# Gated linear attention and expert mix on one core: second-layer weight loads asked for one step sooner, and x tiles' rooms lent to the staging ring

## The chip, the cores and the metric

The kernel runs on one core of one Trainium2 chip. The metric is device time in microseconds (us) of one execution. Before the change it is 2355.21 us, the median of three runs that lie between 2354.76 and 2355.55 us.

The core has a matrix engine (PE, with its weight loads shown apart as PEld), a vector engine (DVE), an activation engine (ACT), a general engine (POOL) and a sync engine (SP). Here SP does nothing but issue DMA transfers, strictly in the order of its instructions: a transfer that has to wait for an engine holds all transfers behind it.

## The reference, cut to what matters

The input `x` is 2048 tokens by 512. Two results are mixed token by token with a sigmoid gate.

```python
g = sigmoid((x * gate_w).sum(-1, keepdims=True))
a = linear_attention(x, wqkv, wo)          # 32 heads of 16
gates = softmax(x @ w_gate)                # 8 experts, all 8 are kept (top 8 of 8)
b = sum(gates[:, e] * (silu(x @ w1[e]) @ w2[e]) for e in range(8))   # w1: 512x1792, w2: 1792x512
return g * a + (1 - g) * b
```

All of it is float32. Nearly all of the arithmetic is in the two products of the experts.

## The kernel before, in words

**Arithmetic.** Each float32 operand is split into a high part and a low remainder, and a product is made of three matmuls (high by high, high by low, low by high): `mm3`, lines 57 to 60, so lines 58, 59 and 60 carry almost all PE work. Both layers use a seven-product scheme for two-by-two blocks in place of eight products; the products are called P1 to P7 and run in the order P1, P7, P2, P4, P6, P5, P3.

**Stages.** First `keys` (the keys and values of the attention, the sums of x that the scheme needs). Then one long loop in `experts`, over slots `u` from 0 to 869. Slot `u` belongs to group `g = u // 7` and step `k = u % 7`. In a slot PE does the first layer's product of group g (`up`: six matmuls into the PSUM tiles `a`, `b` or `c`) and, from slot 58 on (`LAG` = 58), one tick `n = u - 58` of the second layer (`tick`: six matmuls into the PSUM tiles `p`). Slots before 58 hold the first layer alone, and these are the "first stage" in what follows. A group is one pair of 128-column blocks of an expert's first layer; there are 116 groups: the experts for the first half of the tokens (58 groups with two of attention queries), then the same for the second half.

**Preparing weights.** For the first half of the tokens, `prep(g + 1, k)` splits the raw weights `rm` of the next group. The first layer's operands go to the tiles `o`. The second layer's operands are prepared four pieces a group, named by `n` = 0 to 3, into staging tiles: ACT writes the high half (`high2`, and `first(0)` for piece 0), DVE the low half (`low2`, line 219; line 249 for piece 0), and SP stores them to DRAM (`stash`, line 186, `w2stash<-ws`). Pieces 0 and 1 are begun at k = 1, piece 2 at k = 5 and piece 3 at k = 6; piece 0 is stored at k = 2, piece 1 at k = 3, piece 2 at k = 6, and piece 3 at the next group's k = 0. In the trace ACT's part is line 63 `ws<-rm`.

The staging tiles come from a ring of two rooms, tag `ws`. A room can be written again only when the stores of its last piece have landed. While `u < LAG - 8` = 50, pieces 0 to 2 are put into the rooms of the tiles `ho` instead (they appear as `wx`), which the second layer doesn't need yet (`m.spare`, and `ws_tile` in `prep`).

**Loading them back.** `load_w2(i)` (line 782, `w<-w2stash`, 512 KB) brings the two operands of ticks 2i and 2i + 1 into one tile `w`. Until slot 824 (`NU + 12`) these tiles have three rooms, so tile i takes the room of tile i - 3. The condition in the loop asks for tile i at the end of tick 2i - 4. The transfer waits on SP for the last matmul that reads tile i - 3. That matmul is in tick 2i - 5, or in tick 2i - 4 where item 2i - 5 is the first or the sixth of its product (`STEPS`: in these places a tick takes half of two items).

**The order of the work.** It is written out by hand: within a slot `other()` (preparing, splitting, loads of raw weights) is issued ahead of `mid()` (the tick and its evictions), and the loads of `w` follow at the end of the slot. Each engine's queue keeps that order.

**Other users of the rooms in question.** The tag `xs` has two rooms. The two tiles of x(3,1) hold them in `keys`. In the loop, `high` takes one for every sixth hidden operand (n = 5, 11, ...; issued from slot 59 on), and `load_wb` one for each expert's gate row (from slot 74 on).

**The turn to the second half.** In groups 57 and 58 (about 1120 to 1150 us) SP also brings back fourteen x tiles of 512 KB (`x_next`, line 698, `n<-xstash`), and from there on raw weights are the smaller tiles `rs`.

Of the kernel before, what the change touches and what calls it, by code (L numbers as in the profile page):

```python
# [42 lines left out]
def gated_mix_kernel(ctx: ExitStack, tc: tile.TileContext, xT, x, wk, wv, wqkv_q, wo, wm, out):  # L43
# [89 lines left out]
    weights(m)  # L133
    keys(m)
    experts(m, misc)


# [440 lines left out]
def experts(m, misc):  # L578
# [6 lines left out]
    NU = 7 * NG  # L585

    LAG = 44 + 14
# [3 lines left out]
    END = m.A[1].t0  # L591
# [4 lines left out]
    def ho_tile(name):  # L596
        return hp.tile([P, 2, TB], F32R, name=name, tag="ho", bufs=5)

    def out_tile(name):
        return hp.tile([P, TB], F32, name=name, tag="ot", bufs=4)  # L600

# [25 lines left out]
    def spill():  # L627
        while spills and spills[0][0] < m.now:
            _, dst, src, to = spills.pop(0)
            m.phi_last(dst, src)  # L630
            nc.gpsimd.dma_start(to, dst)
# [92 lines left out]
    def differ(u):  # L724
        if u % 7 == 1 and 7 < u < NU + 7 and groups[u // 7 - 1][0].e < E:
            t12, t22 = (raw[u // 7 - 1, f, 1] for f in range(2))
            v.tensor_sub(t12, t22, t12)
        for pairs, offs in ((NPAIR, (None, 6, 15, 29)), (2, (-3, -1, 1, 5))):
            for kind, off in enumerate(offs):
                if off is None or not 0 <= u - LAG - off < END:  # L730
                    continue
                part, prod, q = place(u - LAG - off)
                if part.n == pairs and prod == "P1":
                    difference(kind, part, q)
# [3 lines left out]
    def high(n):  # L738
        part, prod, q = place(n)
        s = blocks(part, q)[SRC[prod]]  # L740

        if END <= n < END + 7:
            h = m.x_tile(f"ho{n}")
        elif END + 7 <= n < END + 10:
            h = [r_tile(f"ho{n}{c}", F32R) for c in range(2)]
        elif n < END and n % 6 == 5:
            h = m.x_tile(f"ho{n}", "xs")
        else:
            h = ho_tile(f"ho{n}")
        if not isinstance(h, list):  # L750
            h = [h[:, c] for c in range(2)]
        act_copy(h[0], s)
        hop[n] = h, s

    def low_h(n):
        h, s = hop[n]
        v.tensor_sub(h[1], s, f32(h[0]))  # L757
        hop[n] = h
# [90 lines left out]
    def tick(n):  # L849
        part, prod, k = place(n)  # L850
        first = prod in ("P1", "P7")
        for q, sub in STEPS[part.n][k]:
            i = n - k + q
            if q == 0 and first:
                pb[BANK[prod], sub] = ps_tile(f"p{n}_{sub}", "dn")
            w = w2s[i // 2][:, i % 2]
            ds = slice(sub * P, (sub + 1) * P)
            h = hop[i]
            assert not isinstance(h, tuple)
            mm3(pb[bank_of(part, prod), sub], w[:, 0, ds], w[:, 1, ds], h[0], h[1], q == 0 and first, q == part.n - 1)  # L860
        if k >= part.n - 2:
            evict(part, prod, k - part.n + 2)
# [87 lines left out]
    def queries_load(i):  # L950
        if i % 2 == 0:
            Q.az = m.raw_tile(f"az{i}", F32R)
            Q.z = Q.az[:, :2 * KT * NH].rearrange("p (c f) -> p c f", c=KT)
            Q.spread = Q.az[:, 2 * KT * NH:2 * KT * NH + D].rearrange("p (c f) -> p c f", c=KT)
            Q.un = Q.az[:, 2 * KT * NH + D:2 * KT * NH + 3 * D].rearrange("p (j t) -> p j t", j=2)
            nc.sync.dma_start(f32(Q.az[:, :2 * KT * NH]), m.zcd)
            nc.sync.dma_start(f32(Q.az[:, 2 * KT * NH:2 * KT * NH + D]), m.spd)
        Q.d = m.raw_tile(f"pq{i}").rearrange("p (c t) -> p c t", c=KT)
        for c in range(KT):
            nc.sync.dma_start(Q.d[:, c], m.pqd[i // 2, i % 2, c])  # L960
# [27 lines left out]
    def queries_last(i, s):  # L988
        if 0 <= s < KT:
            if s == 0:  # L990
                Q.ps = ps_tile(f"dn{i}", "a")
            for j in range(2):
                nc.tensor.matmul(Q.ps[:2 * NH, :], Q.z[:, s], Q.un[:, j], start=(s == 0 and j == 0),
                                 stop=(s == KT - 1 and j == 1))
        elif 14 <= s < 14 + KT:
            Q.ps = ps_tile(f"n{i}_{s}", "a")
            nc.tensor.matmul(Q.ps, Q.spread[:, s - 14], Q.un[:, 0], start=True, stop=True)
# [34 lines left out]
    def rows_first(i, k):  # L1032
        if k == 0 and i % NTT == 0:
            W.acc = m.raw_tile(f"acc{i}").rearrange("p (c t) -> p c t", c=KT)
            W.r = m.raw_tile(f"row{i}").rearrange("p (c t) -> p c t", c=KT)
            for dt in range(KT):
                nc.sync.dma_start(W.acc[:, dt], m.acct[0, i // NTT, dt])
                sums[0, dt, i // NTT] = W.acc[:, dt]
        elif k == 2:
            W.ps = ps_tile(f"o0{i}", "a")  # L1040
            turn(W.ps, 0, i, range(KT), True)
        elif k == 4:
            rows_out(W.ps, 0, i, W.r[:, i % NTT])
# [47 lines left out]
    loaded, highs, lows = 3, 0, 0  # L1091
    ROWS0 = 105
    for u in range(LAG + NTICK):
        m.now = u
        n = u - LAG
        g, k = divmod(u, 7)


        query = [(i, n - part.t0) for i, part in enumerate(m.beside) if -3 <= n - part.t0 < 20]

        def mid():
            if n >= 0:
                tick(n)
            for i, s in query:
                queries_last(i, s)
            if 0 <= g - ROWS0 < NHT and k == 2:
                rows_first(g - ROWS0, k)

        m.spare = ho_tile if u < LAG - 8 else None

        def other():
            nonlocal lows, highs
            if k == 0:
                if u > 0:
                    prep(g, 7)
                m.load(g + 2)
            prep(g + 1, k)
            while lows < min(n + 4, highs, END):
                low_h(lows)
                lows += 1  # L1120
            differ(u)
            while highs < min(n + 5, END):
                high(highs)
                highs += 1
            for _, do, *what in sorted(AHEAD.get(n, ()), key=lambda step: step[0]):
                do(*what)
            for i, s in query:
                if s == -3:
                    queries_load(i)
                queries_first(i, s)  # L1130
            q, s = divmod(u - 7 * WP, 21)
            if 0 <= q < 2 and s == 0:
                m.load_wp(q)
            if 0 <= q < 2 and s > 2 and s % 2:
                if s < 19:
                    m.prep_wp(q, (s - 3) // 2)
            if 0 <= g - ROWS0 < NHT and k != 2:
                rows_first(g - ROWS0, k)
            spill()

        if u < NU + 3:
            up(g, k, mid, other)
        else:
            other()
            mid()
        if u == 5:
            state()
        if u == 6:
            state_last()
        if u in (7, 8, 9, 10):  # L1150
            fold(u - 7)
        if u in (0, 2, 59, 60, 62):
            gates((0, 2, 59, 60, 62).index(u))
        if u == 67:
            gate_rows()
        if u == 7:
            normaliser()
            misc.close()
            m.w2p = ctx.enter_context(tc.tile_pool(name="w2p", bufs=1, side="right", reuse_waits="tile"))
        if u == 74:  # L1160
            load_wb(m.parts[0])
        if n > 7 and n - part_of[n].t0 == 3 and part_of[n].e < E:
            load_wb(part_of[n])
        while loaded < END // 2 and loaded <= (n + (4 if u < NU + 8 else 9)) // 2:
            load_w2(loaded)
            loaded += 1
        if g == m.G1 - 1 and k != 1:
            x_next(max(k - 1, 0))
        if g == m.G1 and k == 1:
            x_next(6)  # L1170
        for part, at in ((m.A[0], -18), (m.A[1], -64)):
            i, odd = divmod(n - part.t0 - at, 2)
            if 0 <= i < 8 and not odd:
                load_query(part, i)

        at = n - END
        if at in range(-38, -3, 5):
            load_w2(END // 2 + (at + 38) // 5)
        if at in (-9, -4, 3):
            load_sums(*{-9: (0, range(KT)), -4: (1, (2, 3)), 3: (1, (0, 1))}[at])  # L1180
        if at in (10, 11):
            for i in range(2):
                rows(2 * (at - 10) + i)
        if at == 12:
            for dt in (2, 3):
                columns(dt, "bc"[dt - 2])
# [41 lines left out]
```

## Time and profile before

| What | Value |
|---|---|
| median of three runs | 2355.21 us |
| these runs | 2354.76, 2355.21, 2355.55 us |
| the profiled execution, its own time | 2354.44 us |
| its span, first to last instruction | 2352.7 us |
| outside the span | 1.7 us |

The busy time of the engines by stage, from the sums over stretches of the span (us):

| Stretch of the span | Length | PE | DVE | ACT |
|---|---|---|---|---|
| 0 to 110: keys | 110 | 108.53 | 78.13 | 68.02 |
| 110 to 190: first stage, slots before 58 | 80 | 76.28 | 69.45 | 63.72 |
| 190 to 1120: both layers, weights still prepared | 930 | 929.20 | 785.79 | 602.73 |
| 1120 to 2240: both layers, stored weights reused | 1120 | 1117.17 | 799.73 | 633.92 |
| 2240 to the end | 112.7 | 107.89 | 78.58 | 51.12 |

How to read it: a row of the timeline gives the start, the length, the engine, the line of the kernel, the operation and the tiles (written<-read, numbers left out), and at the end, in brackets, how long the engine had been idle before it and what ended that. "SPq" are transfers as SP issues them; neighbours of one kind are drawn together (x2, x4). Matmuls overlap: one lasts 0.39 us in the rows, but the next starts 0.23 us after it, so what PE loses at a place is the distance between two starts less 0.23 us. "PEclk" is the clock that PE was granted, 1.00 being full.

### The profile page before, as it was taken

The numbers are of one execution on the slowest core, as the hardware profiler recorded it, in microseconds if no ns is written. First come the engines' busy times: TensorE is split into PE (matmuls) and PEld (weight loads), VectorE is DVE, ScalarE is ACT, GpSimd is POOL, SyncE is SP. The second block draws the span as 40 slices with busy tenths as digits, with TensorE's granted clock in tenths as the row PEclk, the third lists the DMA queues.
The fourth block names the chain that finished last, engine by engine and source line by source line (L and its number), as shares of the span: only waits on it lengthen the run. The fifth ranks groups of instructions, "written<-read, shape, count | busy, mean of one in ns | idle before, by whom it ended". The sixth has DMA issues, their size and how long they took to land.

```text
span 2352.7 us, 31317 instructions
## 1 busy us (share of the span) xinstructions
PE 2339.1 (99%) x10492; PEld 1934.0 (82%) x10492; DVE 1811.7 (77%) x3102; ACT 1419.5 (60%) x2655; POOL 158.6 (7%) x222
## 2 busy tenths in 40 slices
PE   9999999999999999999999999999999999999999
PEld 8877888888888888888788888888888888888887
DVE  6798888888888888888677768776676777766666
ACT  6686666666666666666555555555565655555553
POOL 2101000000000000000000000000011000000101
PEclk9999999999999999999999999999999999999999
DMA  7897888988888898888745455665557646565566
GB/s 230 240 308 248 273 274 257 280 261 267 264 270 276 260 292 252 266 271 251 281 137 176 147 176 152 176 191 143 160 165 190 183 148 176 161 163 168 162 219 209
DMA packets 299346, 513.23 MB, mean 218 GB/s; under 512 B 24353, under 2 KB 193841, under 8 KB 298801
## 3 DMA queue, kind: packets, MB, share of 16 engines
q1 hardware_dynamic: 274992, 464.10, 59.5%
q0 software_dynamic: 23344, 46.49, 10.7%
q8 instruction: 82, 1.34, 0.2%
q14 instruction: 80, 0.65, 0.1%
q10 hardware_dynamic: 848, 0.66, 0.1%
HBM read 343.43 MB, written 163.52 MB: 215 GB/s over the span
## 4 chain that ended last, share of the span: by engine, by line
PE 94%; DMA 3%; DVE 1%; SPq 0%; issue 0%; ACT 0%; POOL 0%; DVEq 0%; ACTq 0%; POOLq 0%
PE p L58 15%; PE p L60 15%; PE p L59 15%; PE a L58 8%; PE a L60 8%; PE a L59 8%; PE c L58 4%; PE c L59 4%; PE c L60 4%; PE b L60 2%; PE b L58 2%; PE b L59 2%; PE g L451 2%; DMA w<-w2stash 2%; PE y L58 1%; PE y L60 1%
## 5 line engine op out<-in xcount | busy, mean ns | idle before, releaser
L58 PE MATMUL p<-ho,w 128*128 128x512 f32 x1620 | 632.3, 390 | 4.5 <-DMA w<-w2stash 3.5
L60 PE MATMUL p<-ho,w 128*128 128x512 f32 x1620 | 630.9, 389 | 0.0
L59 PE MATMUL p<-ho,w 128*128 128x512 f32 x1620 | 630.7, 389 | 0.0
L757 DVE TENSOR_TENSOR ho<-s,ho 128x512 fp32r<-128x512 f32 x784 | 537.4, 686 | 59.4 <-ACT ho L63 55.9
L63 ACT ACTIVATE ho<-s 128x512 fp32r<-128x512 f32 x784 | 487.2, 622 | 22.1 <-PE p L60 10.0
L58 PEld LDWEIGHTS p<-ho,w 128*128 128x128 f32 x1620 | 304.3, 188 | 71.8 <-DMA w<-w2stash 5.1
L60 PEld LDWEIGHTS p<-ho,w 128*128 128x128 f32 x1620 | 304.3, 188 | 63.5
L59 PEld LDWEIGHTS p<-ho,w 128*128 128x128 f32 x1620 | 304.4, 188 | 63.0
L687 DVE TENSOR_TENSOR s<-c,s 128x512 f32<-128x512 f32 x116 | 80.2, 692 | 202.3 <-PE c L60 186.4
L63 ACT ACTIVATE o<-rs 128x512 fp32r<-128x512 f32 x224 | 129.1, 576 | 171.9 <-PE a L60 111.3
L63 ACT ACTIVATE o<-rm 128x512 fp32r<-128x512 f32 x240 | 137.7, 574 | 109.4 <-PE a L60 80.5
L63 ACT ACTIVATE s<-a 128x512 f32<-128x512 f32 x116 | 69.5, 599 | 147.6 <-PE a L60 139.1
L616 ACT ACTIVATE s<-b 128x512 f32<-128x512 f32 x112 | 67.1, 599 | 128.0 <-PE b L60 115.4
L616 ACT ACTIVATE s<-s 128x512 f32<-128x512 f32 x224 | 138.7, 619 | 8.8 <-DVE s L693 5.4
L63 ACT ACTIVATE ws<-rm 128x512 fp32r<-128x512 f32 x206 | 113.9, 571 | 40.2 <-DMA w2stash<-ws 35.0
L205 DVE TENSOR_TENSOR o<-rm,o 128x512 fp32r<-128x512 f32 x180 | 123.0, 683 | 0.1
L205 DVE TENSOR_TENSOR o<-rs,o 128x512 fp32r<-128x512 f32 x168 | 114.5, 681 | 0.6 <-ACT o L63 0.6
L219 DVE TENSOR_TENSOR ws<-rm,ws 128x512 fp32r<-128x512 f32 x156 | 106.9, 685 | 3.3 <-ACT ws L63 3.3
L693 DVE TENSOR_TENSOR s<-a,s 128x512 f32<-128x512 f32 x116 | 80.0, 690 | 33.1 <-PE a L60 32.8
L63 ACT ACTIVATE b<-a 128x512 f32<-128x512 f32 x116 | 67.1, 579 | 61.0 <-PE a L60 61.0
L63 ACT ACTIVATE s<-c 128x512 f32<-128x512 f32 x116 | 69.1, 596 | 25.6 <-PE c L60 25.6
L812 POOL DMA_DIRECT2D acct<-c x30 | 25.6, 852 | 799.1 <-DVE c L806 631.8
(320 smaller groups left out, 4533.8 us busy)
## 6 DMA issues: line engine op xcount, KB each, us to landing
w<-w2stash SPq DMA_DIRECT2D x403, 512.0 KB, 4.5
w2stash<-ws SPq DMA_DIRECT2D x362, 256.0 KB, 3.4
rm<-wm SPq DMA_DIRECT2D x228, 256.0 KB, 5.2
rs<-wm SPq DMA_DIRECT2D x108, 256.0 KB, 3.2
wb<-wgtd SPq DMA_DIRECT2D x16, 512.0 KB, 6.4
acct<-c POOLq DMA_DIRECT2D x30, 256.0 KB, 5.9
acct<-d POOLq DMA_DIRECT2D x30, 256.0 KB, 5.9
acct<-k POOLq DMA_DIRECT2D x30, 256.0 KB, 5.5
```

Of the source, the lines that this page charges most:

```text
L58: nc.tensor.matmul(ps, wh, xh, start=start, stop=False, skip_group_check=True)
L59: nc.tensor.matmul(ps, wh, xl, start=False, stop=False, skip_group_check=True)
L60: nc.tensor.matmul(ps, wlo, xh, start=False, stop=stop, skip_group_check=True)
L63: nc.scalar.activation(dst, src, AF.Copy, scale=scale, bias=bias)
L205: v.tensor_sub(two(o, 1), src, f32(two(o, 0)))
L219: v.tensor_sub(two(w, 1), src, f32(two(w, 0)))
L451: nc.tensor.matmul(ps, xk((0, 0, 1)[j], tb, k, tt * P, (tt + 1) * P), gw[g][:, (0, 1, 0)[j], k, :], start=(k == 0 and j == 0), stop=(k == ...
L616: nc.scalar.activation(dst, src, AF.Silu)
L687: v.tensor_add(sn[g, 2], bank[g, "c"], sn[g, 2])
L693: v.tensor_add(sn[g, 3], bank[g, "a"], sn[g, 3])
L757: v.tensor_sub(h[1], s, f32(h[0]))
L812: nc.gpsimd.dma_start(m.acct[part.h, j, dt], s, accum_op=ALU.add)
```

## The change: what it does

Two edits in the loop of `experts`. The first lets pieces 0 to 2 of the second layer's weights that are prepared in slots 50 to 56 go to the two rooms of the tag `xs` (slots below 50 have the `ho` rooms as before, and from slot 57 on all four pieces use the ring). In slots 50 to 56 the group being prepared is group 8, so it is that group's pieces 0, 1 and 2. The second raises the look-ahead of the loads of `w` from 4 to 5 in all slots below `NU + 8` = 820: tile i is asked for at the end of tick 2i - 5, one slot sooner. No instruction is added or removed; PE, ACT, DVE and POOL keep their orders, and on SP the loads of `w` stand further ahead.

```diff
@@ experts
+    def xs_tile(name):
+        return m.x_tile(name, "xs")
+
...
-        m.spare = ho_tile if u < LAG - 8 else None
+        m.spare = ho_tile if u < LAG - 8 else xs_tile if u < LAG - 1 else None
...
-        while loaded < END // 2 and loaded <= (n + (4 if u < NU + 8 else 9)) // 2:
+        while loaded < END // 2 and loaded <= (n + (5 if u < NU + 8 else 9)) // 2:
             load_w2(loaded)
             loaded += 1
```

The function that picks the room of a piece, unchanged:

```python
def ws_tile(n):
    w = ws[g, n] = m.spare(f"wx{g}_{n}") if m.spare and n < 3 else o_tile(f"ws{g}_{n}", "ws", 2, D)
    return w
```

## The prediction, made before the changed kernel ran

> **What bounds the kernel now.** First the head of the page, then the view of waits for PE, whole and for one stretch.
>
> ```profile
> span 2352.7 us, 31317 instructions
> PE 2339.1 (99%) x10492; PEld 1934.0 (82%) x10492; DVE 1811.7 (77%) x3102; ACT 1419.5 (60%) x2655; POOL 158.6 (7%) x222
> ...
> PE p L58 <- DMA w<-w2stash: 3.5, 4, 2.0
> PE a L58 <- DVE s L693: 3.1, 2, 2.4
> ...
> PE c L58 <- ACT s L63: 0.6, 1, 0.6
> ```
>
> PE is busy 99% of the span, so a change that removes no matmul can give back only what PE waits. The view names four waits for loads of `w` (3.5 us), two on DVE's `s` (3.1 us) and one on ACT's `s` (0.6 us). The edits aim at just these: the second at the loads, the first at the other two. So the gain is small and each place can be followed by itself. I read them one by one in PE's timeline; the loss at a place is the distance between two starts less the usual step, which two rows of the third group show (1143.14 to 1143.37, 0.23 us).
>
> ```profile
> 385.81 0.39 PE L60 MATMUL a<-t3h,o 128*128 128x512 f32 x1
> 386.31 0.50 PE L58 MATMUL p<-ho,w 128*128 128x512 f32 x1
> ...
> 919.34 0.39 PE L60 MATMUL a<-t3h,o 128*128 128x512 f32 x1
> 920.42 0.50 PE L58 MATMUL p<-ho,w 128*128 128x512 f32 x1 [0.70 <-DMA w<-w2stash]
> 920.76 0.39 PE L59 MATMUL p<-ho,w 128*128 128x512 f32 x1
> ...
> 1143.14 0.39 PE L59 MATMUL c<-n1l,o 128*128 128x512 f32 x1
> 1143.37 0.39 PE L60 MATMUL c<-n1h,o 128*128 128x512 f32 x1
> 1143.97 0.47 PE L58 MATMUL p<-ho,w 128*128 128x512 f32 x1 [0.22 <-DMA w<-w2stash]
> ...
> 1149.31 0.39 PE L60 MATMUL a<-n3h,o 128*128 128x512 f32 x1
> 1151.66 0.79 PE L58 MATMUL p<-ho,w 128*128 128x512 f32 x1 [1.96 <-DMA w<-w2stash]
> ...
> 1845.48 0.40 PE L60 MATMUL a<-n3h,o 128*128 128x512 f32 x1
> 1846.52 0.49 PE L58 MATMUL p<-ho,w 128*128 128x512 f32 x1 [0.65 <-DMA w<-w2stash]
> ```
>
> Losses: 0.50 - 0.23 = 0.27 at 386; 1.08 - 0.23 = 0.85 at 920; 0.37 at 1144; 2.12 at 1151.7; 0.81 at 1846. After each, the step to the next matmul is 0.11 us longer as well (0.34 from 920.42 to 920.76). The wait at 1151.7 has a tail, seen in the sums over stretches:
>
> ```profile
> 1151.68:1155.09 3.41, 3.41 (x8) 2.73 (x9) 0.00 (x0) 0.00 (x0) 0.00 (x0) 0.50 0.95 377
> 1155.09:1158.50 3.41, 3.41 (x16) 2.83 (x16) 2.15 (x4) 1.68 (x3) 0.00 (x0) 1.00 0.09 37
> ```
>
> Right after it PE is granted half its clock for 3.41 us, and does 8 matmuls where the next stretch has 16: 1.7 us lost. The five places cost 0.27 + 0.85 + 0.37 + 2.12 + 0.81 = 4.4 us, the longer second steps at four of them 0.4, the slow clock 1.7 (it holds the second step of the fifth): 6.5 us.
>
> **Part one: loads of w one step sooner.** It adds no transfer and no byte; 403 loads move ahead on SP. What do they gain at the five places? SP's issues around three of them:
>
> ```profile
> 375.85 1.03 SPq L168 DMA_DIRECT2D rm<-wm  x2
> 376.92 1.05 SPq L176 DMA_DIRECT2D rm<-wm  x2
> 378.07 0.41 SPq L782 DMA_DIRECT2D w<-w2stash  x1
> ...
> 1137.51 0.32 SPq L698 DMA_DIRECT2D n5h<-xstash  x1
> 1138.79 0.32 SPq L698 DMA_DIRECT2D n5l<-xstash  x1
> 1140.01 1.62 SPq L168 DMA_DIRECT2D rs<-wm  x2
> 1142.63 0.33 SPq L782 DMA_DIRECT2D w<-w2stash  x1
> ...
> 1834.40 0.83 SPq L168 DMA_DIRECT2D rs<-wm  x2
> 1835.32 2.92 SPq L782 DMA_DIRECT2D w<-w2stash  x2
> ```
>
> The load that PE waits for at 386.31 is issued at 378.07, behind four loads of `rm`. One step sooner it stands ahead of these four and of the two stores of piece 3 before them, so it is issued at least 378.07 - 375.85 = 2.2 us sooner, against a loss of 0.27. At 920 the same pattern costs 0.85: also covered. At 1846 the load passes the two loads of `rs` at 1834.40: their issue alone takes 0.9 us, their bytes come on top, against 0.81.
>
> The tight place is 1151.7. There SP issues a 512 KB transfer every 1.28 us (1137.51 to 1138.79), so the transfers are limited by their own rate, and only a place in the line counts. The load of 1142.63 moves ahead of `n5h`, `n5l` and two `rs` of half the size: three times 1.28 = 3.8 us. It needs 2.12 plus the 0.37 that PE would come sooner because 1144 is gone, 2.5 in all. On the other side, an earlier load of `w` now waits on SP for PE ahead of `n1h`, which may leave the line empty for a moment; 3.8 - 2.5 = 1.3 us of emptiness are to be had before the wait comes back. So I let all 6.5 us go. Bounds: nothing (the loads wait for the same tick as before) and 6.5; I take 6.5, because the loads named pass several transfers each, and only where the room's last reader is in the later tick, two in seven, does a load gain nothing.
>
> **What part one adds.** A load that waits on SP for PE now holds the stores behind it, and the ring behind those stores feeds ACT. The nearest rows:
>
> ```profile
> 514.80 3.11 SPq L186 DMA_DIRECT2D w2stash<-ws  x3
> 518.02 3.59 SPq L782 DMA_DIRECT2D w<-w2stash  x2
> ...
> 523.47 0.62 ACT L63 ACTIVATE ws<-rm 128x512 fp32r<-128x512 f32 x1
> ...
> ACT ws L63 <- DMA w2stash<-ws: 30.5, 38, 2.0
> ...
> PE p L58 <- DMA w<-w2stash: 2.9, 3, 2.0
> ```
>
> In the new order the first load of the second row stands ahead of the last two stores of the first. Two issues take about 1.0 us (the row at 375.85), so these two began at 517.91 - 1.0 = 516.9; behind the load, issued at 518.02 in 0.4 us (the row at 378.07), they go at 518.4, 1.5 us later. ACT's write at 523.47 needs their room, so it can be late by up to that. Such an order comes once in two groups, 14 slots of 12 matmuls by 0.23 us, 38 us: 930 / 38 = 24 times in the stage from 190 to 1120. At about 1 us each, between nothing and somewhat over the 1.5, that is some 24 us more of waiting on ACT. The last two rows are the views of waits from 195 (ACT) and 190 (PE) to 1160: ACT already waits 30.5 us for this ring, up to 2.0 us at once, and PE waits for nothing but `w`. So ACT's waits of that size don't reach PE: they are shorter than one slot (12 matmuls by 0.23 = 2.7 us). I take 0, with half of the 24 us as the bad end and no gain possible, since nothing is waited for there.
>
> **Part two: two rooms of xs.** It is to remove ACT's waits for the ring in slots 50 to 56. ACT, DVE, PE and SP there:
>
> ```profile
> 178.66 0.63 ACT L63 ACTIVATE ws<-rm 128x512 fp32r<-128x512 f32 x1 [2.22 <-DMA w2stash<-ws]
> 184.44 0.63 ACT L63 ACTIVATE ws<-rm 128x512 fp32r<-128x512 f32 x1 [2.31 <-DMA w2stash<-ws]
> ...
> 185.10 0.69 DVE L219 TENSOR_TENSOR ws<-rm,ws 128x512 fp32r<-128x512 f32 x1 [0.98 <-ACT ws L63]
> ...
> 186.31 0.69 DVE L693 TENSOR_TENSOR s<-a,s 128x512 f32<-128x512 f32 x1
> ...
> 178.29 11.75 SPq L186 DMA_DIRECT2D w2stash<-ws  x7
> ...
> 180.31 0.50 PE L58 MATMUL c<-x11h,o 128*128 128x512 f32 x1 [0.59 <-ACT s L63]
> 187.06 0.50 PE L58 MATMUL a<-t6h,o 128*128 128x512 f32 x1 [2.37 <-DVE s L693]
> ```
>
> The rows in order: ACT waits 2.22 us for piece 1's room, which makes PE wait 0.59 at 180.31 (0.76 lost). ACT waits 2.31 for piece 2's room until 184.44; DVE's piece 2 follows at 185.10, in DVE's order `s` (line 693) at 186.31, and with its end PE goes on at 187.06. The first wait goes: piece 1 has a fresh room. The second does not: `xs` has two rooms for three pieces, so piece 2 gets the room of piece 0, as it did in the ring, and waits for the same store. That store is the first of the seven at 178.29, and nothing ahead of it in SP's order changes. So 184.44, 186.31 and 187.06 stay, PE reaches the second wait 0.76 us sooner and stands there 0.76 us longer (3.1). The gain is moved, not kept: 0. The other end of its price is both waits gone, 0.8 + 2.5 = 3.3. I take 0, because the view shows which store ends the wait. The borrowed rooms are given back to `high`'s operand from slot 59 on, after these stores; nothing is queued there.
>
> [...]
>
> **The sum.** Against the profiled execution's own 2354.44 us: -6.5 + 0 + 0 = 2347.9. The median of the runs, 2355.21, lies 0.77 above that execution; I carry this over: 2348.7 us.
>
> **The rivals.**
> - The longer wait at 187 brings a stretch at half clock, as 1.96 us did at 1151: 1.7 us back, 2350.4. For it: 3.1 us is longer than either wait seen. Against: 2.37 there did not. [...]
> - Both waits of the first stage go: 2348.7 - 3.3 = 2345.4. Against it stands piece 2's room.
> - The change does not do what it says where it counts: the load at 1151.7 stays late, because SP's line is full, and only the places at 386, 920 and 1846 go (0.27 + 0.85 + 0.81 + 0.3 = 2.2): 2353.0. For it: the rate-limited line there.
> - Slower: SP stands still for PE ahead of the stores of piece 1, ACT waits for the ring in every second group, and half of the 24 us reaches PE: 2348.7 + 12 = 2360.7. It decides from the point where one of ACT's waits grows past a slot, 2.7 us. Against it: PE waits for nothing of ACT or DVE from 190 to 1160 now.
>
> **How the numbers follow.** Chances: forecast 0.50, half clock 0.12, both waits gone 0.10, load still late 0.16, slower 0.12. A measurement tells this kernel from no change at about 0.2%, 4.7 us, so faster means below 2350.5. That takes the forecast nearly whole (0.47), half of the half-clock case (0.06) and the third case (0.10): 0.63. Slower 0.12, within 0.2% the rest, 0.25. The likeliest case alone holds 2346.5 to 2350.5; the range reaches down to the case of both waits gone and up over no change, into the lower part of the slower case, 2344.5 to 2357.
>
> **What would show it.** Right: in the view of waits, PE's row for `w<-w2stash` is gone or below 0.5 us, no half clock near 1150, and one PE wait on DVE's `s` of about 3.1 us at 187 while the one at 180 is gone. ACT's row for `w2stash<-ws` stays near 30 us or grows by up to 24 while PE shows no new wait on ACT or DVE. Wrong: a PE wait near 1150 that stays, a wait at 187 that shrinks, or PE waits on `b`, `c`, `a` or `ho` between 190 and 1120.

## The result, and the profile after

| | before | after |
|---|---|---|
| median | 2355.21 us | 2350.24 us |
| lowest and highest of 13 runs each | 2351.84 to 2357.21 | 2349.28 to 2351.55 |
| the profiled execution | 2354.44 us | 2350.77 us |

The ratio is 0.9981, with a 95% interval of 0.9973 to 0.9990: some 0.2% faster, 5.0 us by the medians, where 6.5 had been forecast. The head of the page and the whole view of waits for PE, of the changed kernel:

```profile
span 2349.1 us, 31301 instructions
PE 2338.4 (100%) x10492; PEld 1935.4 (82%) x10492; DVE 1811.9 (77%) x3102; ACT 1419.3 (60%) x2655; POOL 158.7 (7%) x222
...
PE a L58 <- DVE s L696: 3.9, 2, 3.2
PE idle L515 <- POOL ones L423: 1.4, 1, 1.4
PE p L58 <- DVE d L844: 0.6, 1, 0.6
```

The row for `w<-w2stash` is gone, and so is the one for ACT's `s`. The row for DVE's `s` has grown from 3.1 to 3.9 us, its longest wait from 2.4 to 3.2. (Lines behind the edit stand three further down: 693 is now 696, 782 is 785.) The sums over the two long stages show what is left there:

```profile
190.00:1120.00 930.00, 930.00 (x4102) 769.93 (x4101) 786.54 (x1314) 602.83 (x1137) 47.52 (x63) 1.00 0.86 267
1120.00:2240.00 1120.00, 1120.00 (x4953) 924.76 (x4953) 802.69 (x1407) 636.17 (x1165) 69.53 (x91) 1.00 0.57 172
```

PE is busy from end to end (it missed 0.80 and 2.83 us of these stretches before). Why the loads are in time now is seen in SP's timeline at two of the places:

```profile
376.33 0.33 SPq L785 DMA_DIRECT2D w<-w2stash  x1
377.25 0.87 SPq L186 DMA_DIRECT2D w2stash<-ws  x2
378.18 1.44 SPq L168 DMA_DIRECT2D rm<-wm  x2
...
1138.65 0.32 SPq L785 DMA_DIRECT2D w<-w2stash  x1
1139.87 0.32 SPq L701 DMA_DIRECT2D n5h<-xstash  x1
1141.16 0.32 SPq L701 DMA_DIRECT2D n5l<-xstash  x1
1142.49 1.61 SPq L168 DMA_DIRECT2D rs<-wm  x2
```

The load that stood behind the stores and the four `rm` stands ahead of them; the one that came after `n5h`, `n5l` and `rs` is issued at 1138.65 rather than 1142.63.

The first stage went the other way. ACT, DVE, SP, PE and a stretch of the clock there, changed kernel:

```profile
176.85 0.93 ACT L63 ACTIVATE wx<-rm 128x256 fp32r<-128x256 f32 x2
185.21 0.63 ACT L63 ACTIVATE wx<-rm 128x512 fp32r<-128x512 f32 x1 [3.46 <-DMA w2stash<-wx]
...
187.08 0.69 DVE L696 TENSOR_TENSOR s<-a,s 128x512 f32<-128x512 f32 x1
...
179.19 8.28 SPq L186 DMA_DIRECT2D w2stash<-wx  x5
...
184.28 0.39 PE L60 MATMUL a<-x00h,o 128*128 128x512 f32 x1
187.82 0.70 PE L58 MATMUL a<-t6h,o 128*128 128x512 f32 x1 [3.15 <-DVE s L696]
...
187.90:191.30 3.40, 3.40 (x8) 2.64 (x9) 3.40 (x7) 3.19 (x8) 0.00 (x0) 0.51 0.59 196
```

Pieces 0 and 1 are written one after the other at 176.85, without a wait. Piece 2 waits 3.46 us for the store of piece 0, which is still the first issue of its row. PE's wait is 3.15 us in one piece, and after it PE runs at half clock: 8 matmuls in 3.40 us, where full speed gives 16 in 3.41 (the stretch after the slow one in the prediction). PE goes on at 187.82 and not at 187.06, since this execution runs 0.87 us later by then: the same matmul of `b` starts at 177.71 us after and at 176.84 before.

With that the profiled execution can be added up. Five waits with what follows them: -6.5. Half clock at 188: +1.7. A third term lies in neither edit, at the very start of the span (first row before, second row after):

```profile
6.21 0.64 PE L451 MATMUL g<-g,x00l 128*128 128x256 f32 x4
```

```profile
7.12 0.64 PE L451 MATMUL g<-g,x00l 128*128 128x256 f32 x4
```

The same matmuls come 0.9 us later, in a part of the program in which both kernels have the same orders. What differs there is when PE gets its full clock. The sums over two stretches, first before, then after:

```profile
1.40:4.80 3.40, 3.35 (x8) 2.70 (x9) 0.15 (x1) 1.61 (x2) 0.06 (x1) 1.00 0.75 231
4.80:7.00 2.20, 2.20 (x18) 1.94 (x17) 1.83 (x5) 1.55 (x4) 0.00 (x0) 1.00 1.04 352
...
1.40:4.80 3.40, 3.35 (x8) 2.67 (x9) 0.16 (x1) 1.61 (x2) 0.06 (x1) 1.00 0.74 221
4.80:7.00 2.20, 2.20 (x11) 1.96 (x10) 1.60 (x5) 1.36 (x4) 0.00 (x0) 1.00 1.02 348
```

Up to 4.80 us both do 8 matmuls in 3.4 us, the pace of half clock. Then the kernel before does 18 in 2.20 us and the changed one 11. By the clock records in the two traces full clock begins at 4.80 us before and at 7.05 after. (PEclk shows 1.00 in these rows since the record starts with the first change of the clock.) As the orders there are the same, I put this term down to the execution and not to the change. Together -6.5 + 1.7 + 0.9 = -3.9; measured 2350.77 - 2354.44 = -3.7.

### The profile page after: what moved, and what is told of

The parts are those of the page before. It is cut to its first block, busy times and chain, and to the rows that moved or that the text cites. A ratio compares the mean times of both kernels' runs of the same rounds, so it can differ in the third digit from the quotient of the medians.

```text
span 2349.1 us, 31301 instructions
## 1 busy us (share of the span) xinstructions
PE 2338.4 (100%) x10492; PEld 1935.4 (82%) x10492; DVE 1811.9 (77%) x3102; ACT 1419.3 (60%) x2655; POOL 158.7 (7%) x222
## 3 DMA queue, kind: packets, MB, share of 16 engines
q0 software_dynamic: 23344, 46.49, 10.8%
## 4 chain that ended last, share of the span: by engine, by line
PE 97%; DVE 1%; DMA 1%; issue 0%; ACT 0%; POOL 0%; DVEq 0%; ACTq 0%; POOLq 0%
PE p L58 16%; PE p L60 16%; PE p L59 16%; PE a L58 8%; PE a L60 8%; PE a L59 8%; PE c L59 4%; PE c L58 4%; PE c L60 4%; PE b L60 2%; PE b L59 2%; PE b L58 2%; PE g L451 2%; DMA w2stash<-w 1%; PE y L58 1%; PE y L60 1%
## 5 line engine op out<-in xcount | busy, mean ns | idle before, releaser
L63 ACT ACTIVATE ws<-rm 128x512 fp32r<-128x512 f32 x203 | 114.7, 573 | 66.2 <-DMA w2stash<-ws 59.3
L63 ACT ACTIVATE b<-a 128x512 f32<-128x512 f32 x116 | 67.1, 579 | 58.1 <-PE a L60 58.0
```

The source lines that it names most:

```text
L63: nc.scalar.activation(dst, src, AF.Copy, scale=scale, bias=bias)
```

## The experiments

Seven more kernels were timed against the kernel before.

**The loads alone.**

```diff
-        while loaded < END // 2 and loaded <= (n + (4 if u < NU + 8 else 9)) // 2:
+        while loaded < END // 2 and loaded <= (n + (5 if u < NU + 8 else 9)) // 2:
```

> The loads of w one step sooner alone, the ring of the staging tiles as before. Theory (the loads carry the gain, the lent rooms carry none and lengthen one wait of PE to 3.15 us, after which its clock is halved): PE waits 0.59 us at 180 and 2.37 us at 187 as before the change, no wait for w is left, and the time is 2348.7, that is 1 to 2 us below the changed kernel's 2350.2. Rival (the lent rooms help as well): the time lies above 2350.2, at 2351 to 2353.

Measured: 2348.06 us (2347.24 to 2349.88), ratio 0.9973 (0.9963 to 0.9984). PE's waits, and a stretch of the clock:

```profile
PE a L58 <- DVE s L693: 3.0, 2, 2.3
PE idle L515 <- POOL ones L423: 1.5, 1, 1.5
PE c L58 <- ACT s L63: 0.6, 1, 0.6
...
188.46:191.87 3.41, 3.41 (x10) 2.65 (x9) 2.96 (x6) 2.04 (x5) 0.00 (x0) 0.52 0.56 170
```

All waits for `w` are gone, both waits of the first stage are there as before. This kernel is faster than the whole change by the medians, 2348.06 against 2350.24; the intervals of the two ratios overlap, so by themselves they leave it open. The granted clock that is listed for each run accounts for the difference. A stretch of 3.41 us at half clock takes, as an estimate, 0.0007 off a run's mean clock (half of 3.41 over 2348). Five of the seven runs of this kernel are at 1.000 and last 2347.24 to 2348.19 us; the two at 0.999 last 2349.55 and 2349.88, some 1.7 us longer. All 13 runs of the changed kernel are at 0.999 or 0.998, and those two lie among them (2349.28 to 2351.55). The profile is of one of the two, and it shows that the slow stretch needs no wait of 3.15 us: here it follows one of 2.28.

**The lent rooms alone.** The edit of `m.spare` and `xs_tile` without the look-ahead.

> The lent rooms alone, the loads of w as before. Theory: the wait at 180 is gone, the one at 187 is 3.15 us and is followed by 3.4 us at half clock; all five waits for w stay; the time is 2355.2 to 2357, no gain. Rival (the rooms take ACT's waits away and with them PE's 3.3 us): 2352.

Measured: 2356.4 us (2354.24 to 2357.6), ratio 1.0008 (0.9999 to 1.0016): no gain, as the theory has it. PE's waits for `w`, its wait at 187 and the stretch around that:

```profile
PE p L58 <- DMA w<-w2stash: 2.8, 3, 2.0
...
187.09 0.80 PE L58 MATMUL a<-t6h,o 128*128 128x512 f32 x1 [3.40 <-DVE s L696]
...
185.80:192.60 6.80, 5.51 (x13) 4.35 (x14) 5.51 (x11) 4.67 (x10) 0.00 (x0) 0.50 0.61 178
```

The wait at 180 has moved into the one at 187, which is 3.40 us long, and here the clock is 0.50 in the mean of the 6.80 us from 185.80, before the wait has ended, to 192.60. One thing came out otherwise than expected: three of the five waits for `w` stayed, and those at 386 and 1846 did not occur, although the loads stand where they stood.

**Two pieces in the lent rooms.** Loads and lending as in the changed kernel, but in slots 50 to 56 piece 2 goes to the ring, in `ws_tile` and in the loop:

```diff
-            w = ws[g, n] = m.spare(f"wx{g}_{n}") if m.spare and n < 3 else o_tile(f"ws{g}_{n}", "ws", 2, D)
+            w = ws[g, n] = m.spare(f"wx{g}_{n}") if m.spare and n < m.lent else o_tile(f"ws{g}_{n}", "ws", 2, D)
...
         m.spare = ho_tile if u < LAG - 8 else xs_tile if u < LAG - 1 else None
+        m.lent = 3 if u < LAG - 8 else 2
```

> The changed kernel, but in slots 50 to 56 only pieces 0 and 1 go to the two lent rooms and piece 2 goes to the ring, whose two rooms are free by then. Theory (the third piece in two rooms is what keeps the wait): both waits of PE in the first stage go (3.3 us), and the stretch at half clock behind them (1.7 us): 2345.2, with ACT writing piece 2 at about 182 rather than 185. Rival (something else holds PE at 187, such as the transfers' rate): the wait only shrinks by a part, 2348 to 2350.

Measured: 2346.08 us (2345.13 to 2346.23), ratio 0.9963 (0.9950 to 0.9975), the fastest kernel of the study; its times lie below all 13 of the changed kernel. ACT's write of piece 2, and PE's whole view of waits:

```profile
181.45 0.62 ACT L63 ACTIVATE ws<-rm 128x512 fp32r<-128x512 f32 x1
...
PE idle L515 <- POOL ones L423: 1.4, 1, 1.4
PE a L58 <- DVE s L696: 1.2, 2, 0.7
PE p L58 <- DVE d L844: 0.6, 1, 0.6
```

Piece 2 is written at 181.45 with no wait before it, and no PE wait of over 0.7 us is left in the loop. So the room of the third piece was what held PE. A wait of 0.52 us is left at 185.00, and the time is 0.9 us above the 2345.2 of the theory. The runs are all at a clock of 1.000.

**The loads sooner at the turn alone.**

```diff
-        while loaded < END // 2 and loaded <= (n + (4 if u < NU + 8 else 9)) // 2:
+        while loaded < END // 2 and loaded <= (n + (9 if u >= NU + 8 else 5 if 392 <= u < 413 else 4)) // 2:
```

> The loads of w one step sooner only in slots 392 to 412, the turn to the second half of the tokens; the ring as before. Theory (each of the five places goes on its own): 2.12 + 0.37 + 0.08 + 1.7 = 4.3 us go at 1144 and 1151, the waits at 386, 920 and 1846 stay: 2351.0. Rival (at the turn the transfers' rate sets the wait, and the gain came of the loads before it): the wait near 1151 stays, 2354 to 2355.

Measured: 2350.43 us (2348.51 to 2352.0), ratio 0.9981 (0.9972 to 0.9990), near the 2351.0 of the theory. PE's row for the loads in it:

```profile
PE p L58 <- DMA w<-w2stash: 0.4, 1, 0.4
```

Both waits at the turn are gone, that at 920 is left. Those at 386 and 1846, which the theory kept, did not occur, with their loads unmoved. So 21 of more than 800 slots give 4.4 of the 6.8 us that the loads give altogether (2354.81 being the median of the kernel before beside these runs).

**Two steps sooner.** The kernel with two pieces, look-ahead 6.

```diff
-        while loaded < END // 2 and loaded <= (n + (5 if u < NU + 8 else 9)) // 2:
+        while loaded < END // 2 and loaded <= (n + (6 if u < NU + 8 else 9)) // 2:
```

> The kernel with pieces 0 and 1 alone in the lent rooms (2346.1), with the loads of w asked for one further step sooner (look-ahead 6 for 5). No wait for w is left to gain, so only the price is seen: SP stands for PE ahead of still more stores. Theory (ACT's waits for the ring, 62 us in all and 1.9 at once with look-ahead 5, stay hidden until one of them outlasts a slot of 2.7 us): ACT's waits for the ring grow past 100 us and past 2.7 us at once, PE starts to wait for ACT or DVE between 190 and 1120, and the time is 2350 to 2365. Rival (the ring has more room than a slot): 2346, PE still waits for nothing there.

Measured: 2434.11 us (2432.42 to 2437.12), ratio 1.0339 (1.0324 to 1.0353). The direction and the mechanism are the theory's, the size is far past its 2350 to 2365. PE's and ACT's waits, then one case in the timelines of SP, ACT and PE:

```profile
PE p L58 <- ACT p L63: 25.4, 9, 4.7
PE c L58 <- ACT s L63: 15.0, 11, 2.9
PE a L58 <- DVE s L696: 9.9, 10, 1.9
...
ACT ws L63 <- DMA w2stash<-ws: 275.7, 117, 8.9
...
363.17 0.33 SPq L785 DMA_DIRECT2D w<-w2stash  x1
363.59 2.09 SPq L186 DMA_DIRECT2D w2stash<-ws  x2
...
368.43 0.63 ACT L63 ACTIVATE ws<-rm 128x512 fp32r<-128x512 f32 x1 [4.80 <-DMA w2stash<-ws]
...
370.73 0.79 PE L58 MATMUL p<-ho,w 128*128 128x512 f32 x1 [2.84 <-ACT p L63]
```

SP holds a load of `w` until 363.17; the stores behind it go at 363.59 and after; ACT, which needs their room, stands 4.80 us; and PE stands 2.84 us for an eviction that ACT could not get to. That is the slower rival of the prediction, one step of look-ahead further on. The 88 us above the kernel with two pieces (2434.11 - 2346.08) are more than these waits, about 50 us. Between the two profiles PE is idle for 59.5 us more (67.1 against 7.6 us of the spans) and busy for 28.1 us longer with as many matmuls; for these the clock gives a part: the 0.992 listed for this execution is, as an estimate, 0.008 x 2432.0 x 2 = 39 us at half clock. Eight waits on transfers of `acct`, 7.5 us, are among the idle time too, which the theory did not have.

**Two pieces, loads as before.** The kernel with two pieces, look-ahead 4.

> Pieces 0 and 1 alone in the lent rooms and piece 2 in the ring, the loads of w as before the change. Theory (the two repairs add up, 2348.1 to 2346.1 being the first stage's share with the new loads): both waits of PE in the first stage shrink to under 0.7 us in all, the five waits for w stay, and the time is about 2 to 4 us below the kernel before, 2351 to 2353. Rival (the first stage's waits only move to the loads of w, which come sooner to PE than they land): 2354 to 2355.

Measured: 2350.29 us (2348.85 to 2351.9), ratio 0.9983 (0.9974 to 0.9991), 4.0 us below the median beside it (2354.33); the theory had 2 to 4.

```profile
PE p L58 <- DMA w<-w2stash: 2.7, 3, 1.9
PE a L58 <- DVE s L696: 1.2, 2, 0.7
```

Three of the five waits for `w` are there, again without 386 and 1846; those of the first stage have shrunk. The two repairs add up: 4.0 here and 6.8 for the loads alone give 10.8, above the 8.7 of both together (2354.81 - 2346.08) by 2.1, within what medians of these runs leave open.

**Lending for one more slot.** The kernel with two pieces, and `xs_tile if u < LAG` in place of `LAG - 1`.

> The kernel with pieces 0 and 1 in the lent rooms (2346.1), the lending extended by one slot (slot 57), so that pieces 0 and 1 of group 9 go there too. ACT's wait at 190.8 for piece 1 of group 9 then falls away, but the lent rooms go on to the hidden operand of slot 59 later. Theory (PE is not held there, the operand has four slots of slack): no change, 2345.5 to 2346.5, PE without a wait on ACT or DVE after 186. Rival (the operand of slot 59 is late): 2347 to 2350.

Measured: 2347.27 us (2346.06 to 2347.58), ratio 0.9967 (0.9955 to 0.9980). No gain; 1.2 us above the kernel with two pieces by the medians, with the two intervals overlapping and both profiled spans at 2344.4 us, so whether it costs anything stays open. The operand of slot 59 did have to wait for a lent room, and PE did not notice:

```profile
194.82 0.63 ACT L63 ACTIVATE ho<-s 128x512 fp32r<-128x512 f32 x1 [5.36 <-DMA w2stash<-wx]
```

## Why the prediction was right, and where it was off

What happened is the first rival of the prediction, to which it gave 0.12, and not its forecast: 2350.24 lies within the range, 1.5 us above the 2348.7, by a term that was taken as nothing.

- **The five waits for w, -6.5 us.** Right in the mechanism. The view of waits has no row for them; the loads alone give 2354.81 - 2348.06 = 6.8 us. That the size agrees so well is partly luck: the waits at 386 and 1846, some 1.3 us of the sum, are missing from all three profiles in which the loads there were left alone (rooms alone, turn alone, two pieces with old loads). They come and go from one execution to another; why is open. (The 403 loads that the prediction moves are all loads of `w` in the trace; by the condition in the loop 381 of them move.) The tight place, 1151.7, went as worked out: the load is issued 4 us sooner, and the look-ahead at the turn alone keeps that gain.
- **The lent rooms, 0.** Right in the mechanism: piece 2 waits for piece 0's store, PE goes on when it did but for the 0.87 us by which the whole execution is later, and the gain at 180 reappears as a longer wait at 187. Shown from both sides: the rooms alone gain nothing, and with the third piece sent elsewhere the wait goes, but for 0.52 us. Of the two waits on DVE's `s` that the prediction counts among those aimed at, one, 0.70 us at 134.89, lies in slots that the edits leave alone; it is in the profile after as well (0.70 at 135.79), and the sum does not use it.
- **The term that was mis-sized** is the one taken as 0 behind that: "2.37 there did not", from which the longer wait was expected to keep the clock. It cost 1.7 us in the profiled execution, and the listed clocks show it in all 13 runs of the changed kernel, and in none of the eleven runs of the kernels in which the loads are early too and piece 2 goes to the ring (two pieces, lending for one more slot). 2348.7 + 1.7 = 2350.4 was the first rival, and 2350.24 was measured. The argument drew on a single row at 187, though the prediction itself quoted 1.96 us at 1151 with half clock behind it; the fair reading of these two rows was that either can happen. The last section has both kinds from more kernels.
- **Stores held behind loads, 0 on PE.** Right, and with the price in waiting nearly as forecast: ACT's waits for the ring from 195 to 1160 rose from 30.5 to 59.3 us, 29 more where 24 were worked out. The row of the changed kernel:

```profile
ACT ws L63 <- DMA w2stash<-ws: 59.3, 64, 2.8
```

  The longest is 2.8 us, a slot's length, and PE has no wait on ACT or DVE after 187.82 until the end of the second stage. With look-ahead 6 the longest is 8.9 us and PE waits 50 us on ACT and DVE. The prediction's point of 2.7 us at once is not what decides, though. With look-ahead 6:

```profile
330.05 0.63 ACT L63 ACTIVATE ws<-rm 128x512 fp32r<-128x512 f32 x1 [5.52 <-DMA w2stash<-ws]
...
967.51 0.63 ACT L63 ACTIVATE ws<-rm 128x512 fp32r<-128x512 f32 x1 [2.51 <-DMA w2stash<-ws]
...
969.21 0.50 PE L58 MATMUL p<-ho,w 128*128 128x512 f32 x1 [0.83 <-ACT p L63]
```

  No wait of PE follows the 5.52 us at 330 until 360.80, while after 2.51 us at 967 PE waits 0.83 us for the eviction of `p` that stood behind ACT's piece. By these two cases it counts what ACT has to deliver next, and not the length of its wait alone.

## What to carry to other kernels

A request that stands in an in-order queue is not free to move: look at what it passes, and at what it then holds up while it waits; one step sooner took 6.8 us away here and a second one added 88. When rooms are lent to a ring, count rooms against pieces in flight: with two rooms for three pieces the third waits for the first, and the wait that was removed ahead of it is only moved. A wait of the matrix engine costs more than its length when the slow clock follows it, 1.7 us more behind the 3.15 us here, so a long wait in one piece can be worse than the same time in two: in the two profiles here 0.59 and 2.37 us apart kept the full clock, and 3.15 us in one piece did not.

## What the runs showed of the hardware

The stretch at half clock does not follow the length of the wait alone. Waits of PE in five kernels, and the clock behind them, from the sums over stretches of the span:

| Kernel, wait of PE | PE goes on at | Stretch | Mean clock | Matmuls in it |
|---|---|---|---|---|
| before, 2.37 us | 187.06 | 187.06 to 190.47 | 1.00 | 15 |
| before, 1.96 us | 1151.66 | 1151.68 to 1155.09 | 0.50 | 8 |
| loads alone, 2.28 us | 187.19 | 188.46 to 191.87 | 0.52 | 10 |
| turn alone, 1.99 us | 187.64 | 187.50 to 190.91 | 0.54 | 8 |
| rooms alone, 3.40 us | 187.09 | 185.80 to 192.60 | 0.50 | 13 |
| the change, 3.15 us | 187.82 | 187.90 to 191.30 | 0.51 | 8 |

Waits of 1.96, 1.99 and 2.28 us had a stretch at half clock from their end or shortly behind it, one of 2.37 us had none; the longest wait of the kernel with two pieces and old loads, 1.9 us, left the listed clock of its execution at 1.000. So waits of 1.9 to 2.4 us went either way in these executions; what decides between them is not shown. In the clock records of the kernel before and of the changed one the slow stretch within the loop is 3.41 us long; with the rooms alone it is 6.8. A whole stretch of 3.41 us loses PE 1.7 us (8 matmuls where the next 3.41 us, in the prediction, have 16); with the rooms alone a part of it fell into the wait itself.

These stretches are also part of what spreads the runs. Of the 38 runs of the kernel before beside the experiments, nine are at a clock of 1.000, with a median of 2352.2 us, 21 at 0.999 with 2354.6, and eight at 0.998 with 2355.4. The groups overlap (2355.59 at 1.000, 2353.26 at 0.999), so it is not the whole of the spread; the kernel with two pieces, without such waits, spreads over 1.1 us (2345.13 to 2346.23).
